# The middle pair of row tiles of batch 0 summed and folded by GpSimd, the outer pair by VectorE, with a new order of the opening's calls

## The chip, the cores and the metric

The kernel runs on one core of one Trainium2 chip. The time is the device time of one launch in microseconds (us): the median of several runs. A profile is one further execution of the same program; its times are given beside it.

## What is computed

```python
# x: 8 x 8 x 512 x 64 (batch, head, row, dim), state: 8 x 8 x 32 x 64
def _attn_ref(x, state):
    scores = scale * np.matmul(x, state.transpose(0, 1, 3, 2))
    ...                                    # softmax over the 32 states: a
    xread = np.matmul(a, state)
    scores2 = scale * np.matmul(state, x.transpose(0, 1, 3, 2))
    ...                                    # softmax over the 512 rows: a2
    sread = np.matmul(a2, x)
    return np.concatenate([xread, sread], axis=2)     # 544 rows a head

def _moe_ref(x, w_ch1, w_ch2):             # x: 8 x 544 x 512
    mixed = np.real(np.fft.fft(np.fft.fft(x, axis=1), axis=2))
    u = x + mixed
    ...                                    # layer norm of u: un
    return u + np.maximum(un @ w_ch1, 0.0) @ w_ch2    # 512 -> 2048 -> 512
```

Heads side by side make the 512 columns. Input and output are f32; the kernel works in bf16 on TensorE.

## The kernel before

The kernel goes through eight batches. Of each batch it makes the attention's reads (xread for 512 rows, sread for 32 state rows), then the Fourier mix, then the layer norm and the two layers of the MLP. The mix is done by matrix products with tables of cosines (TC) and sines (TS). Because cosines are even and sines odd, a row and its mirror image need the same table entry, so the rows are first summed or folded: fewer products remain.

**Recorder and order.** Every engine call goes through a recorder (L21 to L63), which collects the calls into groups and replays the groups in the order that the list ORDER gives (L68 to L132). No scheduler reorders behind it. So each engine and each DMA queue gets its instructions in that order, and each then waits for its own operands only. BANKS (L133 to L140) says in the same way which of six PSUM banks each product takes. All instructions have the helper's line, L63, in the profile, so groups are told apart by tile names.

**The opening.** Batch 0 is written apart (`open_batch`, L718 to L816), as nothing else is there to work on. Its steps: ACT and VectorE cast the loaded state (stb) and x (xin) to bf16; TensorE turns the state (sT, by `turn_state`) and four tiles of x (xTp to xT, by `turn`); `score` makes scores (esp), ACT the exponentials (EE); `read` makes a read of one of four row tiles (xrp, which VectorE scales into XF or XR); `sread` makes the state rows (XQ), which `state_rows` puts into XR through ACT. The four row tiles are rows 0 to 127 and 128 to 255 (XF, k = 0 and 1) and, with rows in reverse, 256 to 383 and 384 to 511 (XR, k = 1 and 0): so the pair k = 1 is the middle pair of row tiles, and the pair k = 0, whose XR also takes the state rows, the outer. Then `even` and `odd` (L804 to L814), both on VectorE and for both pairs at once: Sm is the sum of XF and XR, XE0 are Sm's columns folded by addition, XO0 by subtraction (both are shown as SS, the tile that holds them), and ZB (shown as NN) takes two single columns.

**The mix of batch 0.** `transform(0)` (L841) gives the steps. `begin` opens four accumulators (gp); `low_of` adds products with the state rows (XB), `terms_of(j, part)` products with XE0 and XO0, where `part` is the row pair k; `out_of` copies the sums into G (ACT for even j, VectorE for odd j). `over_d` makes the products along the columns (yp), `add_sums` adds the input and sums for the mean (U), `centre_sums` subtracts the mean (ub), `turn_u` turns the result by TensorE (tp) and copies it into unT, from which the first layer (ph, `layer1`) starts. In the main schedule the calls stand like this, from L1320 on:

```python
    low_of(0, 1), low_of(1, 1)
    state_rows()
    low_of(2, 1), low_of(3, 1)
    even()
    ...
    terms_of(0, 1), terms_of(1, 1)
    odd()
    terms_of(2, 1), terms_of(3, 1)
    terms_of(0, 0)
```

ORDER then decides where each of their calls really lands.

**ACT's tables.** The sine tables TS, TC (`sine_s`, `sine_c`) and TEO (`second_sines`) come from ACT's Sin function, the exponentials from Exp. ACT has to load a table (ACT_TABLE_LOAD) when the next function isn't in the one it holds. The kernel places small calls on a spare tile ("gate") to choose when that happens: a Sin ahead of the state copies, `exp_again` ahead of the exponentials, `sin_table` behind them.

**Fillers.** `warm(n)` issues n small matmuls on zeros.

**Loads.** Batch 0's x comes in parts, two on ACT's queue and the others on SP's (`load_x`); state and the following batches' x are on SP's queue. The weights, w1 and w2 in four quarters each, are issued from GpSimd (`first_weights`, `second_weights`) and are taken by its software queue. `cast_x` and `state_blocks` for batches 1 and 2 run on GpSimd too.

Of the kernel before, what the change touches and what calls it, by code (L numbers as in the profile page):

```python
# [49 lines left out]
class _Engine:  # L50
# [3 lines left out]
    def __getattr__(self, what):  # L54
# [14 lines left out]
        19 62 66 61 9-10 12 1 7 11 2 5 4 3 163 8 49 13 6 298 14 55 15 17 16 50 22 0 75-82 29 143 25 27 26 47 28 38 31 41 23  # L69
        144-145 40 39 32 146-147 30 20 46 21 42 48 148 43-45 149 18 24 34-35 33 37 36 72-74 83-118 130 119 329 120-121 123 122  # L70
        155 131 157 124 156 168 330 172 125 141 170 126 169 171 173 142 176 127-129 133-134 184 178 180 192 68 54 159 69-71 177
        185 193 59-60 58 67 64 316 63 65 187 189 186 135-137 188 138 194 196 195 197 139-140 153-154 216 174 331-332 175 206-210
        212 179 211 181 221 219 213 222 132 150-151 182 152 190 198-199 191 217 214 218 200 263 160 167 201-202 51 265 161
        203-204 267-268 165-166 205 299 162 56 261-262 300 158 264 304 266 297 307 303 302 301 57 228 232 229 220 225-227 224
        233 245 223 244 241 183 215 236-240 252-254 231 235 234 230 276-277 247-248 278-279 246 250-251 259 257 255 269 256 272
        249 242-243 258 271 274 284 270 273 317 312 310 309 319 315 314 313 311 318 280-283 285 290 292-293 291 294 275 286 288
        323 322 287 327 326 320 289 321 328 343 324 341 325 345 339 347 340 348 355 333 337 353 378 351 335 386 354 352 346 387
        361 360 342 338 344 385 379 362-365 367 308 260 366 368 52 296 358 382 381 398 356 390-391 380 383-384 521 392-393 396
        394 439 401 400 399 336 357 359 397 334 402-404 406 405 408 407 409 522 413-414 505 523-524 410 415 412 411 441 525 305
        371 370 369 373 422 374 419 375 426 424 420 423 53 526 421 417-418 459 457 349 376 455 453 461 476 465 388 463 473 469  # L80
        467 460 395 350 440 462 456 454 377 458 464 470 468 466 389 472 488 474 480 518 451 481 445-446 449 482 450 487 484 491
        442 492 447 485 496 475 477-478 443 448 495 500-501 506 429-430 428 427 452 591 493 486 479 483 529 536 497 516 498 489
        517 502 499 490 578 164 306 579 507 503 574 527 504 471 508 372 576 580 528 575 416 577 433 432 435 437 434 431 436 543
        582 512 532 519 530 494 583 514 444 520 531 550 533 539 537 589 509 540 538 560-563 510 555 544 556 545 511 438 546 549
        772 547 553 548 559 552 557 554 584 558 598 592 534 585-586 630 622 600 564 569 567 601 606 614 587-588 593 602-603 573
        568 572 570-571 607-608 596 595 597 594 609-610 621 611 613 612 616-617 625 618 627 626 620 619 604 541 624 632 637 599
        535 551 631 615 605 590 623 638 542 652 677 633 641 639 635 565 634 642 640 636 646 661 668 628 566 653 662 678 647 649
        671 654 648 655 670 663 669 664 684 689 685 690 680 682 650 644 659 672 629 683 658 681 667 651 688 693 645 673 660
        714-715 751 704 736-737 757 761 716-717 701 656 700 740 699 295 698 718 728 727 729 657 730 733 732 731 581 674-675
        694-695 679 767 762 782 708 774-775 768 922 745 744 705 771 742 769 741 746 743 738 752 739 754 756 706 763-764 758 755  # L90
        753 776-777 709 778 783 779-780 791 786 790 794-795 787 789 788 702-703 676 713 796 697 765 818 812 864 784 792 802 797
        804 816 814 871 759 808 719 820 766 813 865 819 793 803 785 798 815 805 817 760 809 821 830 823 711 725 720 710 825 726
        712 707 722 806 810 873 799 828 734 880 837 723 721 826 824 827 735 800 781 801 747-748 849 862 842 831 872 807 874 829
        881 836 835 846 850 838 840 839 841 811 863 845 843 852 870 724 773 770 851 750 844 866 858 856 875 911 832 893 877 884
        882 892 833 883 876 857 696 853 859 867 887-888 919 904 886 902 907 974 908 889-890 912 903 921 665-666 891 822 896 691
        847 895 848 899 898 897 900-901 692 686 643 687 954 932 914 878 909-910 920 894 955 928-929 934 968 834 960 957 959 925
        923-924 879 1102 941-942 970 980 996 963 917 976 905 1035 991 987 939 969 975 997 1046 981 933 906 1036 964 918 992 940
        930 913 931 935 943 916 915 937 944-948 938 971 965 949 966 986 950 977 988 967 953 952 951 978 984 993 1103 927 936 958
        973 926 962 961 956 1047 989 982 1007 985 994 979 990 983 1008 1048 1003 998 1012 1040 1009 1053 1022 1024 1058 1101
        1000 999 1001 1014 1005 1013 1004 1002 1041 1006 1054 1010 1025 1011 1060 1086 1061 1051 1067 1077-1078 1049 1062  # L100
        1015-1016 1063 1023 1059 1018 1027 1052 1064 1070 868 1071 1073-1074 1072 860 869 861 854 1075-1076 855 1079-1080 1050
        1087 1140 1017 1026 1031 1042 1280 1105 1104 1107 515 1134 1139 1137-1138 1106 1082 1037 1097-1098 1055 1119 1146 1084
        1236 1112 1069 1065 1056 1083 1099-1100 1066 1088 1038 1091 1113 1132 1108 1148 1094 1213 1166 1164 1110 1120 1019 1028
        1147 1237 1133 1114 1089-1090 1115-1116 1118 1117 1126 1122 1095 1081 1121 1124 1123 1141 1096 1143 1142 1130 1125 1111
        1144 1158 1205 1154 1092 1193 1162 1168 1127 1160 1149 1032 1085 1214 1165 1043 1109 1159 1167 1155 1206 1093 1194 1169
        1145 1131 1128 1161 1163 1174 1231 1207 1188 1219 1150 1175-1177 1151 1178 1057 1039 1136 1135 513 1179 1232 1220
        1181-1182 1180 1279 995 1020-1021 425 1029 1238-1239 1183 1172 1225 1156 1264 1191 1229 1226 1157 1192 1230 1185 1208
        1173 1171 1186 1189 1240 1184 1241 1190 1187 1243 1201 1196 1224 1197 1281-1282 1129 1068 1153 1200 1285 1195 1283-1284
        1209 1215 1255 1245 1256 1260 1227 1288 1257-1258 1244 1228 1247 1274 1261 1198 1030 1242 1044 1248 1250 1254 1249 1170
        1253 1199 1045 1033-1034 1275-1276 1221 1233 1335 1272 1277 1222 1289 1259 1265 1304 1273 1278 1308 1268 1305 1270  # L110
        1290-1291 1315 1252 1251 1267 1316 1292 1266 1234 1286 1321 1331 1297 1364 1343 1319 1327 1337 1376 1310 1407 1262 1293
        1269 1294 1296 1306 1295 1322 1312 1314 1332 1344 1299 1313 1300 1303 1301 1309 1342 1361 1302 1271 1202 1210 1287 1336
        1298 1320 1328 1216 1377 1365 1395 1408 1311 1338 1333 1325 1339 1359 1329 1340 1334 1326 1330 1317 1354 1402 1390 1360
        1318 1391 1403 1263 1398 1378 1435 1409-1410 1345 1357 1356 1355 1358 1379 1411 1399 1412 1348 1346-1347 1349 1367 1372
        1352 1368 1353 1307 1323 1235 1223 1386 1380 1366 1371 1413 1419 1421 1211-1212 1420 1217 1424-1425 1203-1204 1218 1341
        1423 1422 1369-1370 1392 1404 1426-1427 1416 1400 1362 1446-1447 1396 1384 1350 1428 1436 1429 1440 1393 1405 1363 1373
        1397 1351 1385 1401 1454-1455 1481 1491 1431 1441 1474 1461 1536 1450 1492 1482 1475 1462 1451 1439 1438 1418 1448-1449
        1456-1457 1468 1437 1458 1460 1459 1463 1476 1478 1464 1414-1415 1432 1445 1465-1466 1452 1512 1570 1499 1501 1489 1443
        1453 1477 1467 1444 1430 1497 1493 1469 1479 1537 1442 1513 1500 1490 1502 1498 1494 1472 1470 1473 1480 1516 1483 1507
        1495 1485 1524 1563 1519 1517-1518 1496 1520 1486 1508 1510 1509 1504 1511 1394 1406 1521 1505 1433 1538 1484 1527 1381  # L120
        1532 1525 1514 1564 1387 1528 1434 1515 1506 1523 1539 1522 1544 1554 1567 1558 1556 1550 1557 1540 1546 1471 1526 1531
# [50 lines left out]
def kernel(  # L172
# [545 lines left out]
    def open_batch():  # L718
# [92 lines left out]
        def odd():  # L811
            nc.vector.tensor_sub(XO0[:, :, 0:256], Sm[:, :, 0:256], Sm[:, :, 512:256:-1])
            nc.vector.tensor_sub(XO0[:, :, 256:512], Sm[:, :, 256:0:-1], Sm[:, :, 256:512])
            nc.vector.memset(XO0[:, :, 0:1], 0.0)  # L814
# [740 lines left out]
```

## Time and profile before

| | |
|---|---|
| runs | 288.75, 287.68, 288.82 us; median 288.75 |
| profiled execution | 287.47 us, of which the span of the core's records is 285.7 |
| granted TensorE clock | 0.997 |
| last exponential of batch 0 ends (ACT) | 11.56 us |
| XQ, the state rows before they are turned (VectorE) | 13.49 to 13.78 |
| Sm, both pairs (VectorE) | 15.48, 0.69 us |
| first-axis products gp end (PE) | 19.37 |
| first matmul of layer 1, ph (PE) | 22.39 |
| state 0 has landed | 3.00 |
| tiles of x 0 have landed | 4.34, 5.96, 7.30, 8.34 |
| quarters of w1: issued by GpSimd | 11.59, 15.48, 16.29, 17.02 |
| quarters of w1: landed | 17.49, 21.00, 23.55, 26.08 |

Times inside an execution count from the start of its span. PE is TensorE, DVE VectorE, POOL GpSimd, and SP the engine that issues most of the DMAs. A row of a timeline has the start, the duration, the engine, the operation with output and inputs, and in brackets the idle time before it with what ended it. A row with "x3" stands for three instructions that follow each other without a gap; their durations overlap where an engine pipelines. The chain of work is followed back from the last instruction of the execution to whatever released each step; what is not in it had time to spare.

### The profile page before, as it was taken

To read this page: it belongs to the slowest core of one execution; us is meant where nothing else is said; L and a number is where in the kernel's file an instruction comes from. 1 tells how busy PE (TensorE), PEld (TensorE's weight loads), DVE (VectorE), ACT (ScalarE), POOL (GpSimd) and SP (SyncE) were. 2 spreads that over 40 slices of the span, in tenths; PEclk is the share of its full clock that TensorE was granted. 3 is DMA by queue.
4 is the path that set the end of the run, shared out by engine and by line. 5 is a ranking of instruction groups with operands and counts; after the bars stand their busy time and mean duration, and the time that the engine had idled before them with its cause. 6 is when DMAs were issued, how large, how long until landed. Compare 5 with 4: busy or idle time off the path is not lost.

```text
span 285.7 us, 6835 instructions
## 1 busy us (share of the span) xinstructions
PE 275.2 (96%) x2615; PEld 199.0 (70%) x2644; DVE 210.6 (74%) x554; ACT 162.0 (57%) x327; POOL 92.5 (32%) x227
## 2 busy tenths in 40 slices
PE   7899999999999999999999999999999999999993
PEld 6788985555655778567758777576577667686882
DVE  6877777468899988985798688959766578224892
ACT  7897656746936576368377564586566653254000
POOL 8392476670660033502712119006200028000000
PEclk9999999999999999999999999999999999999998
DMA  8999959966366346861379640413201520978366
GB/s 156 185 181 190 202 95 181 197 146 153 83 157 103 93 116 156 107 170 25 80 169 194 149 94 19 98 53 65 84 0 48 151 65 18 182 149 136 92 162 184
DMA packets 110972, 34.91 MB, mean 122 GB/s; under 512 B 101996, under 2 KB 106476, under 8 KB 110940
## 3 DMA queue, kind: packets, MB, share of 16 engines
q1 hardware_dynamic: 100220, 28.72, 47.5%
q0 software_dynamic: 4224, 4.19, 9.7%
q10 hardware_dynamic: 6496, 1.57, 2.6%
q8 instruction: 20, 0.33, 0.5%
q14 instruction: 12, 0.10, 0.1%
HBM read 22.41 MB, written 14.02 MB: 128 GB/s over the span
## 4 chain that ended last, share of the span: by engine, by line
PE 87%; DVE 7%; DMA 2%; issue 1%; ACT 1%; SPq 1%; DVEq 0%
PE ph L63 39%; PE poA L63 18%; PE poB L63 13%; PE gp L63 4%; PE po L63 3%; PE yp L63 2%; DVE U L63 2%; DMA xs<-in_x_dram 2%; PE esp L63 2%; PE eTp L63 1%; PE xrp L63 1%; DVE XR L63 1%; PE xfp L63 1%; DVE ot L63 1%; SPq L63 1%
## 5 line engine op out<-in xcount | busy, mean ns | idle before, releaser
L63 PE MATMUL ph<-unT,w 128*128 128x512 bf16 (+2 forms) x743 | 127.9, 315 | 1.4
L63 ACT ACTIVATE hT<-ph 128x512 bf16<-128x512 f32 x128 | 72.1, 596 | 76.6 <-PE ph L63 76.3
L63 PEld LDWEIGHTS <-w 128*128 128x128 bf16 x768 | 64.3, 98 | 42.5 <-issue 0.6
L63 PEld LDWEIGHTS <-hT 128*128 128x128 bf16 x632 | 60.4, 98 | 14.8 <-issue 0.3
L63 DVE SCALAR_TENSOR_TENSOR ot<-poA,rstd,U 128x256 f32<-128x256 f32 (+1 forms) x46 | 21.7, 475 | 16.5 <-PE poA L63 13.8
L63 POOL CAST xin<-xs 128x2048 bf16<-128x2048 f32 (+3 forms) x14 | 14.5, 1046 | 48.5 <-PE poA L63 20.3
L63 PE MATMUL poB<-w,hT 128*128 128x256 bf16 x224 | 28.2, 273 | 0.0
L63 POOL TENSOR_TENSOR rstd<-rstd,mhalf 128x1 f32<-128x1 f32 x34 | 20.3, 604 | 1.1
L63 POOL TENSOR_TENSOR rstd<-mv,epst 128x1 f32<-128x1 f32 x14 | 2.8, 211 | 42.9 <-DVE mv L63 42.9
L63 ACT CAST G<-gp 128x288 bf16<-128x288 f32 (+2 forms) x31 | 12.8, 477 | 5.6 <-PE gp L63 5.3
L63 ACT ACTIVATE ub<-U,S 128x512 bf16<-128x512 f32 (+1 forms) x22 | 15.1, 706 | 1.5 <-DVE U L63 1.3
L63 PE MATMUL po<-w,hT 128*128 128x512 bf16 x60 | 15.4, 379 | 0.2
L63 PE MATMUL poB<-TA,SA 128*128 128x256 bf16 x120 | 15.5, 273 | 0.1
L63 PE MATMUL poA<-TA,SB 128*128 128x256 bf16 x120 | 15.6, 273 | 0.0
L63 DVE SCALAR_TENSOR_TENSOR U<-yp,XF 128x2 f32<-128x2 f32 (+1 forms) x24 | 10.0, 419 | 7.5 <-PE yp L63 5.3
L63 DVE SCALAR_TENSOR_TENSOR ot<-poB,rstd,ot 128x256 f32<-128x256 f32 x30 | 14.2, 478 | 1.0 <-PE poB L63 0.8
L63 PE MATMUL poA<-TC,hT 128*128 128x256 bf16 (+1 forms) x120 | 14.5, 265 | 0.1
L63 POOL COPY XT<-XR 32x514 bf16<-32x514 bf16 x7 | 4.2, 605 | 31.8 <-DVE U L63 15.8
L63 PE MATMUL poA<-w,hT 128*128 128x256 bf16 x112 | 14.5, 273 | 0.0
L63 ACT ACTIVATE junk<-U,S 128x512 bf16<-128x512 f32 x20 | 14.3, 716 | 0.2
L63 PE MATMUL poA<-TB,hT 128*128 128x256 bf16 x112 | 14.3, 273 | 0.0
L63 DVE SCALAR_TENSOR_TENSOR ot<-poB,rstd,U 128x256 f32<-128x256 f32 x15 | 7.2, 478 | 9.0 <-PE poB L63 9.0
(197 smaller groups left out, 478.3 us busy)
## 6 DMA issues: line engine op xcount, KB each, us to landing
xs<-in_x_dram SPq DMA_DIRECT2D x22, 256.0 KB, 3.8
w<-in_moe_w_ch_dram POOLq DMA_DIRECT2D x8, 512.0 KB, 6.8
out_dram<-ot SPq DMA_DIRECT2D x15, 256.0 KB, 2.4
r_dram<-ot SPq DMA_DIRECT2D x14, 256.0 KB, 2.4
out_dram<-r_dram SPq DMA_DIRECT2D x14, 256.0 KB, 3.7
xs<-in_x_dram SPq DMA_DIRECT2D x8, 192.0 KB, 4.9
xs<-in_x_dram ACTq DMA_DIRECT2D x2, 256.0 KB, 4.7
l_dram<-ot SPq DMA_DIRECT2D x2, 256.0 KB, 2.0
```

The costliest lines, as they stand in the source:

```text
L63: self._rec.add(self._name, lambda: f(*args, **kw), key)
```

## The change

`even` and `odd` take a row pair k and an engine, and work on that pair alone. The pair k = 1 goes to GpSimd, both folds at once, and the pair k = 0 stays with VectorE:

```diff
-        def even():
-            nc.vector.tensor_add(Sm, XF, XR)
-            nc.vector.tensor_add(XE0[:, :, 128:256], Sm[:, :, 256:128:-1], Sm[:, :, 256:384])
-            nc.vector.tensor_add(XE0[:, :, 0:128], Sm[:, :, 0:128], Sm[:, :, 512:384:-1])
-            nc.vector.tensor_copy(XE0[:, :, 128:129], Sm[:, :, 256:257])
-            nc.vector.tensor_add(ZB[:, 2:4, 0:1], Sm[:, :, 128:129], Sm[:, :, 384:385])
-
-        def odd():
-            nc.vector.tensor_sub(XO0[:, :, 0:256], Sm[:, :, 0:256], Sm[:, :, 512:256:-1])
-            nc.vector.tensor_sub(XO0[:, :, 256:512], Sm[:, :, 256:0:-1], Sm[:, :, 256:512])
-            nc.vector.memset(XO0[:, :, 0:1], 0.0)
+        def even(k, eng):
+            m, e = Sm[:, k], XE0[:, k]
+            eng.tensor_add(m, XF[:, k], XR[:, k])
+            eng.tensor_add(e[:, 128:256], m[:, 256:128:-1], m[:, 256:384])
+            eng.tensor_add(e[:, 0:128], m[:, 0:128], m[:, 512:384:-1])
+            eng.tensor_copy(e[:, 128:129], m[:, 256:257])
+            eng.tensor_add(ZB[:, 2 + k, 0:1], m[:, 128:129], m[:, 384:385])
+
+        def odd(k, eng):
+            m, o = Sm[:, k], XO0[:, k]
+            eng.tensor_sub(o[:, 0:256], m[:, 0:256], m[:, 512:256:-1])
+            eng.tensor_sub(o[:, 256:512], m[:, 256:0:-1], m[:, 256:512])
+            eng.memset(o[:, 0:1], 0.0)
...
-    even()
+    even(1, nc.gpsimd)
+    odd(1, nc.gpsimd)
+    even(0, nc.vector)
...
-    odd()
+    odd(0, nc.vector)
```

This makes 1755 groups of calls where there were 1747, and ORDER and the choice of PSUM banks are written anew. From about 36 us on the order is the old one; the opening's differs. Engine by engine, the two programs differ there like this:

- ACT: the four state copies (stb) and the x cast stand ahead of the Sin on the spare tile, not behind it, and the program has five table loads, not four. Three multiplications that make negative tables stand ahead of the copy that puts the state rows into XR. The last load, for Exp, stands ahead of the second half of TEO and the copies into G, not behind them.
- VectorE: the casts of two further tiles of x 0 stand ahead of the sT and xT copies. The first unT copy stands behind an addition for the second tile of U.
- TensorE: the tiles of x are turned before the first scores, and the reads run in the order 2, 3, 1, 0, with 1 and 0 behind the last exponential. The transposes of batch 1's state stand ahead of yp.
- GpSimd: ahead of its part of XB come two casts of x 1 and two quarters of w1; behind it the fold of the pair k = 1 with a third quarter of w1 in it, then the state copies, casts and the mirror table, then the state copies for batch 2, the last quarter of w1 and the first of w2.
- SP: state 1 is loaded earlier, the parts of x 1 come in another order, and the load of state 2 stands behind those of x 2, the first of which waits for a cast on GpSimd.

## The prediction

> **What bounds the kernel now.** I read the busy times first, then the chain that ended last, then the opening engine by engine.
>
> ```profile
> PE 275.2 (96%) x2615; PEld 199.0 (70%) x2644; DVE 210.6 (74%) x554; ACT 162.0 (57%) x327; POOL 92.5 (32%) x227
> ...
> PE 87%; DVE 7%; DMA 2%; issue 1%; ACT 1%; SPq 1%; DVEq 0%
> ```
>
> PE is busy for 275.2 us of 285.7. Its own idle times sum to 5.8 us before the last matmul, 3 of them before 9 us; after the first layer-1 matmul (ph, 22.39) there are only some 2 us (the largest 0.38 at 28.0 and 0.56 at 49.84). So later matmuls don't wait, and the change, which touches only the first 36 us, acts through one thing: when the opening hands PE its steady work. The chain's steps from 0 to 27 us (start, duration):
>
> ```profile
> 3.60 4.75 DMA xs<-in_x_dram
> ...
> 10.06 0.78 PE esp L63 x22
> 12.09 0.70 DVE XR L63
> 13.56 0.23 DVE XQ L63
> 13.83 0.70 PE warm L63 x6
> 14.54 1.59 PE gp L63 x13
> ...
> 16.84 2.53 PE gp L63 x29
> 19.37 0.22 PE warm L63 x4
> 19.59 0.47 PE yp L63 x4
> 20.09 0.71 DVE U L63 x2
> 21.99 0.36 DVE unT L63
> 22.39 1.05 PE ph L63 x16
> ```
>
> The chain runs through scores (esp), exponentials, reads (XR), state rows (XQ), the sums gp and yp. The fold that is moved lies just before the gp row of 16.84. ACT's own timeline of the opening:
>
> ```profile
> 1.90 1.28 ACT L63 ACT_TABLE_LOAD   x1 [1.90 <-issue]
> ...
> 5.78 0.54 ACT L63 ACTIVATE TC<-gen,halfpi 128x288 bf16<-128x288 f32 x1
> 6.32 1.28 ACT L63 ACT_TABLE_LOAD   x1
> 7.61 0.20 ACT L63 ACTIVATE gate<-gate 128x1 f32<-128x1 f32 x1
> 8.24 0.59 ACT L63 COPY xT<-xTp 128x512 bf16<-128x512 bf16 x1 [0.43 <-PE xTp L63]
> 9.81 1.75 ACT L63 ACTIVATE EE<-esp 128x512 bf16<-128x512 f32 x3 [0.48 <-PE esp L63]
> ```
>
> ACT has 0.43 + 0.48 us of idle between the gate and the last exponentials, so it is nearly a bound here already: its last exponential ends at 11.56.
>
> **ACT: one more table load (the largest term).** In the changed program the first ACT work is the four state copies and the x cast; the sine activation that stood ahead of them comes after. So a load of another table stands ahead of the copies, behind their wait for the state (landing at 3.00), and the sine table is loaded after them: five loads instead of four. Before, the first load ran at 1.90 under the wait for data and cost nothing. Stepped with the rows: 3.0 + 1.28 load, four copies of 0.30 to 5.5, cast 0.62 to 6.2, load 1.28 to 7.5, gate, TS and TC to 8.6, load 1.28 to 9.9, gate to 10.1. Before, this point was 7.61 + 0.20 = 7.81. Of the +2.3, 0.9 goes into the idle above. Then xT 10.1, four exponentials at a spacing of 0.5 from 10.6: the last ends at 12.7 (+1.15). The Trainium skill ("ScalarE: Activation LUTs", section "What ACT_TABLE_LOAD costs") puts some 1.38 us of draining onto each load. The rows show none: TC ends at 6.32, where the load starts, and the gate follows at 7.61. By the row the extra load is 1.28, by the rule 2.66 and the exponentials +2.5; I take the row, since this is the same instruction in this place.
>
> **VectorE's order.** The casts of x tile 1 and of the 96-row tile (landings 7.30 and 8.34) now stand ahead of the sT copy, which ends at 9.27 instead of 8.09. Scores wait for sT, so this alone would put the last exponential at 12.0 (+0.43). It lies beside ACT's delay: the later counts, so nothing is added.
>
> **PE's order.** Reads go 2, 3, 1, 0, and reads 1 and 0 both stand behind the last exponential, ahead of sread: about +0.2. XQ ends at 15.1 against 13.78 (+1.36). The transposes of the next batch's state take the place of the four warm matmuls before yp (0.22 each way): nothing.
>
> **The fold.** VectorE's Sm add, two folds and two odd folds fall from two row tiles to one: 0.69 + 2 x 0.25 + 2 x 0.38 become about half. GpSimd gets the other half. It has no such row; the nearest are its two-input adds:
>
> ```profile
> 29.10 0.66 POOL L63 TENSOR_TENSOR XEl<-XT 32x256 f32<-32x256 bf16 x1
> ```
>
> 0.66 for 256 columns, with 0.45 for 128 (XQl<-XEl at 31.50): some 1.8 ns a column and 0.2 fixed. So Sm (514) takes 1.1, two of 128 take 0.9, two of 256 take 1.3, small ones 0.2: 3.5 us. The lower end is 2.5 (all bf16, where the row writes f32), the upper 5 (locked, below). It starts when XF and XR of tile 1 are there, 14.6, and with a weight DMA issue (0.75) and copies between ends at 19.1. PE wants the pieces at 18.2 to 21.5 in my stepping, 0.45 to 1.5 us after each is done. That cover hides it; without it each us of lateness is a us at the end.
>
> The Trainium skill ("SBUF — State Buffer", section "Who interferes with whom") speaks against this: a VectorE operation with two SBUF inputs and a GpSimd operation that reads SBUF shut each other out. The trace agrees:
>
> ```profile
> 172.42 0.68 DVE L63 TENSOR_TENSOR hT<-hT 128x1024 bf16<-128x1024 bf16 x1
> 172.46 1.17 POOL L63 TENSOR_TENSOR XEl<-XT 32x256 f32<-32x256 bf16 x1
> ```
>
> XEl takes 1.17 instead of 0.66 under it; the VectorE row keeps its 0.68 here, and in three such overlaps takes 0.75 to 0.79. In the opening VectorE's own fold (some 1 us of two-input work) meets GpSimd's reads. By the unlocked row the cost is 0; by the rule all of the overlap, 1 us, is lost on one of the two. GpSimd's part fits in the slack up to about 0.5, so I take +0.3, from 0 to +1.
>
> **ACT behind the fold.** The copy that makes the state rows waits for GpSimd's Sm and minus operations and three ACT multiplies now precede it (XR 15.9 to 16.5, before 14.84 to 15.44); the exp table load moves from behind the G copies to ahead of them (18.1 to 19.3, before 19.53), so ub isn't later by it. PE's low gp runs 15.6 to 17.6, then the terms 18.2 to 20.5 (before to 19.37), yp ends at 21.45 (before 20.06: +1.4).
>
> **After yp.** U starts at 21.5 (+1.4); unT now stands behind a U operation of the second tile on VectorE, so the first ph starts at 24.1 (+1.7). That is partly made up: by the 192nd ph the lag is +1.3, by the 231st +1.2.
>
> **The DMAs that are moved.** On GpSimd two casts of x and two w1 quarters go ahead of XB, one w1 quarter stands amid the fold, the last behind the state blocks of batch 2, which wait for a state load behind the x(2) loads on SP's queue; each holds the next. The last w1 quarter lands at 32 to 34 (before 26.08), wanted at about 35.3 (before 34.3); the first two quarters of w2 at 34 to 36 and 40, wanted at 40 and 42.2. So cost 0, with 1.3 to 3 us of slack; a queue later by 2 would turn into a stall on w1 of 0.7 or more. The opening's own loads on SP change places but none that PE waits for lands later by the step.
>
> **Sum.** Lag +1.2 to +1.7 at steady work, I take +1.3, and +0.3 for the shared port: +1.6, own range +1.0 to +2.2. Nothing behind can take it in but the waits of about 0.9 named above. The profiled execution then is 287.47 + 1.6 = 289.1 (span 287.3), and as the median of before is 1.28 above its profiled execution, the forecast is 288.75 + 1.6 = 290.35.
>
> **The rivals.** B, absorbed: the extra load delays the exponentials, but the waits of 0.38 at 28.0 and 0.56 at 49.84 vanish, since what ends them is not delayed. For it: PE's first hundred ph catch up 0.4 in my stepping. Against: the waits after 22.39 are for things that hang on the same chain. It gives +0.6: 289.3.
>
> C, GpSimd becomes the bound: folds at the locked price (5 us instead of 3.5) end 1.5 after their time, and eat the slack of 0.45 at the first piece; the lag grows by 1.0 to 1.5, or the last w1 quarter comes late by the same. For it: the 1.17 row and four things queued behind each other. Against: the VectorE part is only 1 us long. It gives +2.9: 291.65.
>
> D, not slower: GpSimd starts tile 1's fold before the state rows are there, so that PE's gp terms start without the fillers (0.70 at 13.83, 0.11 at 16.13, 0.11 of idle before 16.84): -0.8 at most. It decides if the last exponential ends no more than 0.8 us after 11.56, that is if the first table load runs before the state has landed and its sine load hides in the wait for x (xT is only there at 8.24). Time 288.75 - 0.8 = 287.95 with no lag, 288.75 with 0.8. Against: the order of the instructions, which puts the second load behind the cast.
>
> **How the numbers follow.** A measurement of this kernel can tell about 0.5% from no change, 1.44 us. A (forecast, 290.35) 0.52, B 0.18, C 0.23, D 0.07. The bound for slower is 290.19: two thirds of A (0.34) and all of C make 0.57; the rest of A (0.18), B and a quarter of D make 0.38; what of D gains more than its fillers, 0.05. The range takes B less 0.7 (runs of before differ by 1.1) and C plus 0.75: 288.6 to 292.4; outside are D's faster part and a lock or a late quarter worse than C.
>
> **What would show it.** ACT: five loads, the second sine load near 6.2 to 7.5, the last EE ends near 12.7. DVE: sT near 9.3. POOL: Sm<-XF,XR 128x514 near 1.1 us; much over 1.5 says lock. PE: yp near 21.4, first ph near 24.1, and no wait over 0.3 at the last w1 quarter near 35. It would be wrong if the first load ran at 1.9 without waiting, if the copies shared the sine table, or if the folds took over 5 us.

## The result, and the profile after

The changed kernel takes 290.42 us in the median of 5 runs (290.17 to 291.48), where the kernel before took 288.75 in runs beside it. The medians differ by 1.67 us; the ratio of the runs is 1.0093 with a 95% interval of 1.0072 to 1.0114. A second set of both kernels on one chip gave 290.23 against 287.95, ratio 1.0076 (1.0061 to 1.0091), or 2.2 us. The forecast was +1.6 us (0.55%) and 290.35: the sign is right and the time lies in the range, but by both ratios the loss is larger, by some 0.6 us in the second set. That 290.42 lies so near to 290.35 is in part luck. The forecast was counted from the 288.75 of the kernel before, and in three later sets the medians of that kernel were 287.70 to 287.95.

The profiled execution took 291.48 us, the slowest of the five, with a span of 289.7. The page's busy times and the shares of its chain:

```profile
span 289.7 us, 6847 instructions
PE 276.5 (95%) x2615; PEld 199.2 (69%) x2644; DVE 213.0 (74%) x554; ACT 163.1 (56%) x328; POOL 96.6 (33%) x235
...
PE 69%; POOL 7%; SPq 5%; issue 4%; DVE 4%; DMA 4%; ACT 4%; POOLq 0%; DVEq 0%; ACTq 0%
```

PE's work is nearly the same; the chain has more of other engines in it. Its steps of the opening (start, duration):

```profile
0.72 2.58 DMA gen<-in_state_dram
...
3.37 1.28 ACT L63
...
6.55 1.28 ACT L63
...
8.81 1.28 ACT L63
...
10.78 1.98 ACT EE L63 x4
...
15.23 1.15 POOL Sm L63
...
16.76 0.60 ACT XR L63
17.36 0.02 issue
17.38 0.44 DVE Sm L63
...
17.84 1.35 DVE SS L63 x3
...
20.19 0.30 PE gp L63
...
25.16 1.05 PE ph L63 x16
```

Before, the chain began with the loads of x. In this execution it begins with the load of the state, and goes through three table loads on ACT. Then it passes GpSimd's Sm, ACT's copy into XR, VectorE's Sm and folds. A further execution of the same program, the second profile (span 288.5), has another chain up to ACT's copy:

```profile
4.37 4.33 DMA gen<-in_state_dram
...
8.84 0.29 POOL stb L63
...
13.36 0.65 POOL XB L63
...
14.22 1.16 POOL Sm L63
...
15.76 0.59 ACT XR L63
...
16.38 0.44 DVE Sm L63
...
19.18 0.30 PE gp L63
```

It begins with the landing of batch 1's state at 8.70 and follows GpSimd's queue: casts of batch 1's state and x, w1 issues, its part of XB, Sm. ACT's own list (last exponential, table load, two sines, three multiplications) ends at 15.70 in this execution, and GpSimd's clearing of XB at 15.75; the copy starts at 15.74. So two paths reach this copy almost together, one along ACT and one along GpSimd's queue, and taking time out of one alone leaves the other. ACT and PE show the waits that matter, in the first profile:

```profile
3.37 1.28 ACT L63 ACT_TABLE_LOAD   x1 [3.37 <-DMA gen<-in_state_dram]
...
10.68 2.07 ACT L63 ACTIVATE EE<-esp 128x512 bf16<-128x512 f32 x4
```

```profile
20.19 0.30 PE L63 MATMUL gp<-NN,SS 128*128 128x288 bf16 x1 [0.66 <-DVE SS L63]
```

The first row is the new table load, held by the state's landing; the second has the four exponentials in one block, now without idle time ahead of them. The third is a wait that the kernel before did not have: PE waits for a fold piece of VectorE (0.51 in the second profile).

Milestones of the opening, read from one trace of each kernel (us; "XQ" is its end; "last x cast" is the start of the cast of the 96-row tile, "gp" the end of the first-axis products, "ph" the first matmul of layer 1):

| kernel | state lands | last x cast | last EE ends | XQ | gp | ph |
|---|---|---|---|---|---|---|
| before | 3.00 | 8.46 | 11.56 | 13.78 | 19.37 | 22.39 |
| changed, first profile | 3.30 | 8.63 | 12.75 | 15.55 | 22.02 | 25.16 |
| changed, run again | 2.84 | 8.51 | 12.29 | 14.69 | 21.02 | 24.16 |
| Sin first | 2.88 | 8.28 | 11.78 | 14.21 | 20.69 | 23.83 |
| fold on VectorE | 3.01 | 8.37 | 12.54 | 15.20 | 21.60 | 24.74 |
| order only | 2.91 | 8.46 | 11.96 | 14.40 | 21.09 | 24.22 |
| even first | 3.16 | 8.17 | 12.61 | 15.29 | 20.93 | 24.28 |
| mended | 3.13 | 8.54 | 11.96 | 14.54 | 20.37 | 23.30 |
| load alone | 2.83 | 8.21 | 12.16 | 14.05 | 19.69 | 22.70 |
| fold alone | 2.87 | 8.25 | 11.35 | 13.61 | 20.76 | 25.45 |
| fold, casts ahead | 2.98 | 8.38 | 11.48 | 13.70 | 20.86 | 24.82 |
| released copy | 2.94 | 8.35 | 12.51 | 14.88 | 21.24 | 24.38 |
| released copy, Sin first | 3.15 | 8.18 | 11.59 | 14.19 | 20.57 | 23.50 |
| before, XB work ahead | 2.90 | 8.35 | 11.45 | 13.67 | 19.21 | 22.21 |

### The profile page after: what moved, and what is told of

Read it like the earlier page. It is cut to its first block, busy times and chain, and to the rows that moved or that the text cites. A ratio compares the mean times of both kernels' runs of the same rounds, so it can differ in the third digit from the quotient of the medians.

```text
span 289.7 us, 6847 instructions
## 1 busy us (share of the span) xinstructions
PE 276.5 (95%) x2615; PEld 199.2 (69%) x2644; DVE 213.0 (74%) x554; ACT 163.1 (56%) x328; POOL 96.6 (33%) x235
## 4 chain that ended last, share of the span: by engine, by line
PE 69%; POOL 7%; SPq 5%; issue 4%; DVE 4%; DMA 4%; ACT 4%; POOLq 0%; DVEq 0%; ACTq 0%
PE ph L63 30%; PE poA L63 17%; PE poB L63 13%; SPq L63 5%; DMA xs<-in_x_dram 3%; PE gp L63 3%; POOL xin L63 2%; PE yp L63 2%; ACT L63 1%; POOL stb L63 1%; DVE ot L63 1%; DVE XR L63 1%; DMA gen<-in_state_dram 1%; PE eTp L63 1%; PE esp L63 1%
```

## The experiments

The theory after the first trace was: the table load, and VectorE's folds stretched by GpSimd's. The first rival: only the load. A second, which came up on the way: the new order of the calls, apart from both. Every ratio is to the kernel before on the same chip.

**The changed kernel again.**

> The changed kernel once more, unaltered, so that the others can be compared with it on the same chip and with a second profile. The first profile had the first ph 2.8 us later than before (25.16 against 22.39), and the same lag at the end but for 0.8. If that is the kernel and not the one execution, this profile shows the first ph at 24.8 to 25.2 and the ratio to before is 1.007 to 1.010. Rival (the profiled execution was an outlier): first ph near 24.1 as forecast, ratio 1.005.

Median 290.23 against 287.95, ratio 1.0076 (1.0061 to 1.0091); ph at 24.16. So two executions of one program differ by 1.0 us at this point, and the first profile was on the late side. Of that, 0.46 is the state's landing (3.30 against 2.84). The last exponential ends 9.45 us after that landing in both. Another 0.40 lies between the last exponential and XQ. There VectorE's copy XB takes 0.71 instead of 0.29, where GpSimd's copy of the same size had started 0.04 ahead of it. The last 0.14 lies between XQ and the end of gp. The rival was right on the place of ph, the theory on the ratio.

**The Sin first.** The edit, in ACT's part of ORDER:

```diff
-        33 35-36 34 37 24 72-74
+        24 33 35-36 34 37 72-74
```

> The changed kernel with one call moved back: ACT's Sin on the spare tile stands again ahead of the four state copies, so the program has four table loads. My theory (the table load behind the wait for the state costs 1.15 us at the exponentials, less what VectorE's order of casts holds back by itself, 0.43): the first load at about 2 us, the last exponential ends at 12.0 to 12.1 instead of 12.75, first ph 0.7 earlier than in the changed kernel, total 0.7 less (289.7 where before is 288.75, ratio about 1.003). Rival (the load is covered, the whole loss is in the fold): nothing moves, ratio 1.006.

289.51 against 287.81, ratio 1.0075 (1.0048 to 1.0103). The last exponential ends at 11.78 instead of 12.29 and ph comes 0.33 earlier than in the second profile of the changed kernel. So the last exponential gained 0.51, and the ratio did not move. This is a miss for the theory. The 0.33 at ph cannot be put down to the load either: GpSimd's Sm, too, starts 0.33 earlier (13.89 against 14.22), as batch 1's state landed earlier here, and the chain of this execution runs along GpSimd's queue, as in the second profile. What the load costs in the changed kernel is not shown by this run, since the other path held. ACT's row of the exponentials:

```profile
9.68 2.10 ACT L63 ACTIVATE EE<-esp 128x512 bf16<-128x512 f32 x4 [0.91 <-PE esp L63]
```

With the load gone, ACT waits 0.91 us for scores. In the new order sT stands behind the last x cast, and all tiles are turned ahead of the first scores. In the four kernels with the new order and four loads the last exponential ends 3.4 to 3.5 us after the last x cast starts, in before 3.1. Two of the four (released copy with the Sin first, and mended) have sT ahead of that cast again, and still end 3.41 and 3.42 after it, against 3.50 in the other two. So sT's place is worth some 0.08. The rest fits the place of the scores behind the turn of the last tile: before, one exponential ran at 8.73 and three at 9.81 (1.75 us), now all four run in a row (2.10 us). With five loads the bound is the other one, 9.45 to 9.57 after the state's landing.

**The fold given back to VectorE.**

```diff
-    even(1, nc.gpsimd)
-    odd(1, nc.gpsimd)
+    even(1, nc.vector)
+    odd(1, nc.vector)
```

> The changed kernel in its new order, but the fold of the middle pair is given back to VectorE; five table loads stay. My theory after the trace (GpSimd's adds keep their time and VectorE loses: its four folds take 0.52, 0.29, 0.70 and 0.74 where the twice as wide ones took 0.29 and 0.42; the state rows' copy also waits for GpSimd's Sm): VectorE's folds go back to 0.25 to 0.4 each, the ZB and XB work of GpSimd ends before 15 and the copy into XR starts about 16.2 instead of 16.75; PE's first ph comes 0.8 to 1.5 us earlier than in the changed kernel, ratio to before about 1.002. Rival (only the load counts): VectorE has 0.7 us more to do, ratio 1.006 to 1.008.

290.16 against 287.81, ratio 1.0075 (1.0061 to 1.0089): no gain. The stretching is real. VectorE's rows in the changed kernel's first profile:

```profile
15.58 1.09 DVE L63 TENSOR_SCALAR gen<-gen 128x512 int32<-128x512 int32 x1
...
17.84 1.35 DVE L63 TENSOR_TENSOR SS<-Sm 128x128 bf16<-128x128 bf16 x3
...
19.20 0.74 DVE L63 TENSOR_TENSOR SS<-Sm 128x128 bf16<-128x128 bf16 x1
```

GpSimd's, beside them:

```profile
15.23 1.16 POOL L63 TENSOR_TENSOR Sm<-XF,XR 128x514 bf16<-128x514 bf16 x1 [0.63 <-DVE rcs L63]
...
18.37 0.67 POOL L63 TENSOR_TENSOR SS<-Sm 128x256 bf16<-128x256 bf16 x1
...
19.25 0.60 POOL L63 TENSOR_TENSOR SS<-Sm 128x256 bf16<-128x256 bf16 x1
```

And VectorE with GpSimd's adds taken away:

```profile
15.23 0.38 DVE L63 TENSOR_SCALAR gen<-gen 128x512 int32<-128x512 int32 x1
...
18.15 0.28 DVE L63 TENSOR_TENSOR SS<-Sm 128x256 bf16<-128x256 bf16 x1
...
19.30 0.22 DVE L63 TENSOR_TENSOR SS<-Sm 128x128 bf16<-128x128 bf16 x1
```

The integer operation takes 0.38 instead of 1.09, a 128-column fold 0.22 instead of 0.74, while GpSimd's rows are near what the prediction took from its unlocked rows (1.1 for Sm). But VectorE then has twice the work, and its last piece is as late: from its last Sm to its last fold piece 2.74 us, against 2.76 in the first profile. Nor is the stretch undone in full. With its adds gone, GpSimd's two casts of x 1 come forward to 16.16 and lie beside VectorE's two Sm adds, of which the second takes 0.83 (0.43 in the second profile). So the run shows that giving the work back gains nothing; what the stretch alone costs it does not separate.

**Both undone.**

> The changed kernel with both suspects undone: the Sin stands ahead of the copies again (four table loads), and the fold of the middle pair is on VectorE. What is left is the new order of the calls. My theory: load and fold are not all; last exponential at 11.8 (held by sT), the three multiplications ahead of the copy into XR, VectorE's last folds behind the odd ones and 16 transposes between the two yp still cost, together 0.9 to 1.5 us: first ph at 23.3 to 23.8, ratio 1.003 to 1.006. Rival (load and fold are the whole loss): first ph at 22.4 to 22.8, ratio 1.000 to 1.001.

290.23 against 287.95, ratio 1.0086 (1.0065 to 1.0108), ph at 24.22. The theory did not expect this: with four loads and no GpSimd fold the new order still costs what the change costs. But it does not show the new order by itself. This order is made for a VectorE with half the fold: from its last Sm to its last piece VectorE takes 3.17 us here. And GpSimd's casts of x 1 have again moved into the gap that its fold left:

```profile
15.83 1.51 POOL L63 CAST xin<-xs 128x512 bf16<-128x512 f32 x2
```

```profile
16.02 0.83 DVE L63 TENSOR_TENSOR Sm<-XF,XR 128x514 bf16<-128x514 bf16 x1
```

This Sm takes 0.83 and the fold of 128 columns behind it 0.63, where alone they take 0.43 and 0.22: some 0.8 us on VectorE's list, which PE then waits for. So sharing between the two engines is in this test too, through other calls. The late scores belong to the order alone (the last exponential at 11.96, +0.40), and so does the place in VectorE's list of the piece that PE waits for; how much of the 1.8 at ph the order makes by itself is not shown.

**The load alone**, in the kernel before:

```diff
-        24 34-35 33 37 36 72-74
+        34-35 33 37 36 24 72-74
```

> The kernel before with one call moved: ACT's Sin on the spare tile stands behind the four state copies and the x cast. This adds the table load behind the wait for the state and nothing else. My theory: first load at about 3.0 to 3.3, ACT reaches the exponentials 2.3 us later, 0.9 of it absorbed by its idle times, last exponential at 12.7 to 13.0, first ph and total +1.2 to +1.4, ratio 1.0045. Rival by the rule on draining (each load costs 2.66): last exponential at 14, ratio 1.009. Rival (absorbed): ratio 1.000 to 1.001.

288.26 against 287.81, ratio 1.0015 (1.0006 to 1.0024). The expected 1.0045 is out. ACT's rows:

```profile
2.90 1.28 ACT L63 ACT_TABLE_LOAD   x1 [2.90 <-DMA gen<-in_state_dram]
...
5.97 1.28 ACT L63 ACT_TABLE_LOAD   x1
...
10.10 2.06 ACT L63 ACTIVATE EE<-esp 128x512 bf16<-128x512 f32 x4
...
14.99 0.60 ACT L63 CAST XR<-warm 32x512 bf16<-32x512 f32 x1 [0.22 <-issue]
```

The last exponential ends 0.6 later than before, but the copy into XR starts only 0.15 later (before: 14.84). Before, ACT idles 0.67 ahead of this copy, for a GpSimd clearing that stands behind a cast of another batch's state. This is that row of before:

```profile
14.84 0.60 ACT L63 CAST XR<-warm 32x512 bf16<-32x512 f32 x1 [0.67 <-POOL XB L63]
```

For the copy, that idle time took most of the delay. PE's path takes in less: XQ ends 0.27 later than before, since before the chain between the last exponential and XQ ran through VectorE's reads, and this step takes 1.89 here instead of 2.22. From there PE carries 0.3 on to ph and to its last ph, and the total is 0.45 later. A load costs its 1.28; a load of 2.66, as the rule on draining has it, would have shown at the exponentials, and did not.

**The fold alone**, in the order of before: the change's code, with GpSimd's eight calls put behind the last read of its pair, a w1 quarter ahead, one inside and one behind.

> The kernel before, in its own order of the opening, with the fold of the middle pair on GpSimd from the time that its reads are there (two weight transfers stand inside and behind it, one is issued earlier). No further table load. My theory (the shared port): VectorE's Sm and folds overlap GpSimd's and each stretches by 0.3 to 0.45 us, so that the end of the sums is 0.3 to 1.0 later in spite of half the work, ratio 1.001 to 1.004. Rival (the fold is a gain that the new order spoils): VectorE ends its part 0.7 earlier, PE's products start without fillers, ratio 0.998.

292.12 against 287.81, ratio 1.0129 (1.0107 to 1.015), the slowest of all. Its runs fall into two groups, 290.63 and 290.78 in one and four from 292.08 to 292.16 in the other; the profile is of the first, so some 1.4 us of the median's loss are in no trace and stay open. VectorE and GpSimd start their Sm within 0.4 us:

```profile
15.48 1.04 DVE L63 TENSOR_TENSOR Sm<-XF,XR 128x514 bf16<-128x514 bf16 x1 [0.49 <-ACT XR L63]
```

```profile
15.08 1.16 POOL L63 TENSOR_TENSOR Sm<-XF,XR 128x514 bf16<-128x514 bf16 x1 [0.23 <-DVE XF L63]
```

VectorE needs 1.04 for half the Sm that takes 0.69 whole in before. PE then waits for GpSimd's pieces:

```profile
17.19 0.24 PE L63 MATMUL gp<-NN,SS 128*128 128x144 bf16 x1 [0.27 <-POOL SS L63]
18.29 0.24 PE L63 MATMUL gp<-NN,SS 128*128 128x144 bf16 x1 [0.80 <-POOL SS L63]
```

gp ends 1.4 late; then PE waits 1.6 more for x casts that stand on GpSimd behind the fold. In the old order, in this kernel and the next, rival C of the prediction is true: GpSimd's folds are the bound.

**The fold alone, x casts ahead of the last w1 quarter.**

> The fold alone in the order of the kernel before, once more, with GpSimd's three casts of x 1 directly behind its fold and the last w1 quarter behind them. In the first version the products ended 1.4 later than before (20.76 against 19.37), and the transposes of x 1 then waited 1.6 for casts that stood behind two weight transfers. My theory: the second part goes (first ph at 23.8 to 24.0 instead of 25.45, ratio 1.005), the first, which is the fold's own, stays. Rival (the casts are not what is waited for): first ph stays above 25, ratio 1.011 or more.

290.20 against 287.70, ratio 1.0078 (1.006 to 1.0097). The 1.4 to 1.5 at gp stays, as expected; of the second part about half goes, since the state casts behind the x casts are now late: from gp to ph PE loses 0.94 instead of 1.67, and ph at 24.82 misses the expected 23.8 to 24.0. Against the profiled time of the fold alone, 290.63, this kernel's profile is only 0.3 faster. PE's waits from 15 to 26 us (engine, what it waited for, us in total, times, longest):

```profile
PE sTp L63 <- POOL stb L63: 1.3, 1, 1.3
PE gp L63 <- POOL SS L63: 1.1, 2, 0.8
```

**Released copy into XR.** In the changed kernel, GpSimd's groups 202 and 204 ahead of its Sm (236), VectorE's integer operation (132) ahead of 151.

> The changed kernel with GpSimd's ZB subtraction and XB clearing put ahead of its Sm, so that ACT's copy into XR no longer waits behind Sm, and VectorE's integer operation on 512 columns (1.09 us under GpSimd's Sm, 0.38 when GpSimd does not read) put ahead of the reads. My theory (the chain through GpSimd's Sm, ACT's copy and VectorE's Sm is real): XR copy 0.5 earlier, VectorE's Sm 0.5 earlier at 16.8 instead of 17.4, total 0.4 to 0.6 less than the changed kernel, ratio 1.006. Rival (the folds end last anyway): 0 to 0.1.

290.17 against 287.95, ratio 1.0074 (1.0059 to 1.0089), the same as the changed kernel on that chip. A miss. The copy starts at 15.83, no earlier than the 15.74 of the second profile, and now it is held by ACT's own multiplications; VectorE's Sm starts at 16.44 and its first three fold pieces take 1.95. GpSimd's path is off the chain, and ACT's, which had been level with it, holds the copy in its place.

**The same with the Sin first, sT ahead of the last cast, unT ahead of the second U.**

> As the last one, with the Sin ahead of the copies (four loads), VectorE's sT copy ahead of the last cast as in the kernel before, and the first unT copy ahead of the second tile's U. GpSimd keeps the fold. My theory (load 0.7 to 1, release 0.5, sT 0.3, unT 0.2): first ph at 22.8 to 23.2, ratio 1.001 to 1.003, still not better than before because VectorE's folds stretch under GpSimd's. Rival (the shared port costs nothing once the order is mended): ratio below 0.999.

289.30 against 287.95, ratio 1.0048 (1.0033 to 1.0063); ph at 23.50. About 0.9 less than the changed kernel, though less than expected. Both paths to ACT's copy are shortened here at once, where the Sin first and the released copy, each alone, gained nothing. That fits two paths that end together; as four edits were made in one run, it is not shown which of them counted. PE still waits 0.57 for a fold piece.

**The even half first.** In VectorE's part of ORDER, in the changed kernel:

```diff
-        246 260-262 248 245 247
+        246 245 247 260-262 248
```

> The changed kernel with VectorE's own fold put in another order: the second half of XE0 and its single column ahead of the two subtractions for XO0, as the products of the outer pair want them. My theory: in all kernels with the new order TensorE waits 0.5 to 0.66 us for exactly this piece (its products end 1.9 us after the last fold piece in each of them), so the wait goes and the first ph comes 0.4 to 0.6 earlier than in the changed kernel run again (23.6 to 23.8 against 24.16), ratio about 1.006. Rival (the subtractions then come late and take the wait's place): 0 to 0.1.

289.85 against 287.70, ratio 1.0067 (1.0046 to 1.0088). PE's wait is gone; the chain is PE's own from the last read on:

```profile
15.35 0.70 PE warm L63 x6
16.05 1.96 PE gp L63 x16
...
18.65 0.74 PE gp L63 x10
19.39 0.06 PE warm L63
19.45 1.48 PE gp L63 x17
```

From XQ to the end of gp it takes 5.64 us, where before took 5.59 and the changed kernel 6.33 to 6.47. So with VectorE's pieces in the order in which they are wanted, this stretch of the opening is as long as before in this execution; in the mended kernel, with the same order, it is 5.83. In this execution exponentials and reads were late (state at 3.16), so ph is at 24.28; the total is lower by less than the interval, which neither shows nor rules out the expected 0.5. The mended kernel below differs by this same edit from the one with the released copy and the Sin first: there ph is 0.20 earlier and the ratio lower by 0.0009, also within the intervals.

**All of it.**

> All that was found so far in one kernel, GpSimd keeping its fold: four table loads, sT ahead of the last cast, GpSimd's ZB and XB work ahead of its Sm, VectorE's integer operation ahead of the reads, the even half of the outer pair first, the first unT ahead of the second U. My theory: 0.4 to 0.5 less than the version without the last edit (1.0048), first ph at 23.0 to 23.1, ratio 1.003: not better than before, since VectorE's two-input operations still stretch under GpSimd's. Rival (GpSimd's fold is worth the 0.5 that VectorE no longer does): ratio 1.000 or below.

288.97 against 287.70, ratio 1.0039 (1.0026 to 1.0052), ph at 23.30. About half of the loss is taken back by moving single calls, with GpSimd's fold kept; the expected 1.003 and ph at 23.0 to 23.1 were not reached. What is left at ph, 0.91, lies at the last exponential (+0.40, in part its last x cast, 0.1 late), from there to XQ (+0.36) and from XQ to the end of gp (+0.24), less 0.1 behind it. The other half of this profile's lag arises behind the first ph: it is 1.89 at the last ph.

**The kernel before, with GpSimd's XB work ahead of the cast.**

```diff
-        51 265 161 203-204 267-268
+        51 203-204 265 161 267-268
```

> The kernel before with one GpSimd cast (batch 1's state, waiting for its load to 14.28) and one small clearing moved behind the ZB addition and XB clearing, for which ACT's copy into XR waits 0.67 us. Fold on VectorE as before. My theory: the copy starts about 14.4 instead of 14.84 and VectorE's Sm at 15.2, when its last read is scaled, instead of 15.48: total 0.2 to 0.3 less, ratio 0.999. Rival (the products wait for their tables): 1.000.

287.61 against 287.70, ratio 0.9992 (0.9985 to 1.0000). The copy starts at 14.51 instead of 14.84:

```profile
14.51 0.60 ACT L63 CAST XR<-warm 32x512 bf16<-32x512 f32 x1 [0.45 <-DVE XR L63]
```

It beats the changed kernel clearly, and the kernel before by 0.1% at the edge of what can be told.

## Why the prediction was right in sign and too small

The forecast's lag, step by step, beside the two profiles of the changed kernel:

| step | forecast | run again | first profile |
|---|---|---|---|
| last exponential | +1.15 | +0.72 | +1.18 |
| from there to XQ | +0.2 | +0.2 | +0.6 |
| XQ to the end of gp | -0.2 | +0.74 | +0.88 |
| gp to the first ph | +0.6 | +0.12 | +0.12 |
| first ph to the end, port included | -0.1 | +1.0 | +1.2 |
| sum, on the span | +1.6 | +2.8 | +4.0 |

**The table load** was placed rightly: five loads, the first held by the state, the second sine load at 6.1 to 7.8, the exponentials at 12.3 to 12.75. The row's price of 1.28 held, the rule's 2.66 did not. What the forecast didn't see is that "nothing behind can take it in" is false for the load by itself: the copy into XR lost only 0.15 of the 0.6, and the total 0.45. The term put at 0.43 beside it is there when the load goes (11.96 in the kernel with both undone: +0.40), so its size was right. Its cause was not: sT's place on VectorE is worth some 0.08, and the rest goes with PE turning all tiles ahead of the scores, a term that the forecast does not have. Up to ACT's copy into XR (forecast 15.9, second profile 15.74) the stepping held.

**The fold** is the term that was sized wrongly. The forecast stepped GpSimd's pieces (3.5 us in sum; the trace has 3.7) against PE's needs, found slack, and took +0.3 for the port on top, judging it by GpSimd's slack. GpSimd was on time indeed, and it was VectorE that lost: in the second profile its first three folds take 1.35 and the fourth 0.74. Two things make PE's wait of 0.5 to 0.66 together. One is this stretch. The other is the order of VectorE's own pieces: the second half of XE0 stands behind both subtractions, and PE wants it ahead of them. With the unstretched times (the same seven pieces take 1.04 in the kernel with the fold on VectorE) the last piece would be done near 17.9 in the second profile, an estimate, where PE wants it near 18.5; measured it is done at 19.13. So by this estimate PE would not have waited without the stretch; and in the two kernels with the other order it did not wait at this piece in spite of it. Stepping VectorE's list with the stretched times would have shown the wait.

**From gp to ph** it is 0.12, not 0.6: unT does stand behind a U operation, but U itself starts 0.71 after the end of gp, not 1.0 as stepped.

**The later waits.** The two waits that the forecast gives as 0.38 at 28.0 and 0.56 at 49.84 are 0.21 at 28.40 and 0.39 at 50.45 in the trace of before. The first is gone in every kernel with the new order. The second grows to 0.59 or 0.60 in all of them, while both stay as they were in the four other kernels with the opening of before: so about 0.2 of the loss behind ph comes with the new order.

**After ph** the forecast expected a catching up by 0.4 and no loss later. The catching up was 0.2 (192nd ph +1.56 in the second profile). Later 0.45 were lost on a transposing DMA; this is PE's row at 70 us in the second profile:

```profile
70.39 0.29 PE L63 MATMUL esp<-sT,xT 128*128 128x64 bf16 x4 [0.45 <-DMA xT<-xin]
```

This DMA had been issued at 66.75 and landed at 70.35. The one behind it landed at 71.80, 3.15 after its counterpart before (68.65), while PE was 1.6 late: SP's queue had lost more than PE. Another 0.4 to 0.5 is between the last ph and the end. Which of these other losses belong to the new order and which to the execution is not settled: kernels with an early ph lose more behind it (1.0 in mended, 0.55 in the second profile, 0.16 in the order alone), the first profile has its late wait at 85 us (0.40) instead, and the load-alone kernel keeps its +0.31 unchanged to the last ph.

**The weights** were right: the last w1 quarter landed at 31.2 and 32.5 in the two profiles (forecast 32 to 34), and no wait of PE was for it.

**The rivals.** B (absorbed) is true of the load by itself in part, and in another place: the two later waits stay in the load-alone kernel. It is not true of the change. C is true of the fold in the old order only. D (a gain) was never there: PE's fillers ahead of the products stayed, and in the even-first kernel the time from XQ to gp is before's. The likeliest case came near by a sum in which some terms were too high and others too low: in the second profile 0.43 and 0.48 less at two steps, 0.94 and 1.1 more at two others. That the time came out so near is luck in this respect too.

## What to carry to other kernels

Where a change comes with a new order of calls, undo the named parts and keep the order: here that kept the whole loss, and neither named part would have told. Look then at what slid into the gap: with the fold gone, GpSimd's casts came forward and stretched VectorE's adds in its stead. Where two paths end together, undoing either shows nothing; undo both. Step every engine's list of pieces in the order in which their consumer takes them, also the engine that gets less work, and with the durations that it has beside the other engine: here neither the order nor the stretch made the wait by itself. And a delay upstream is to be followed to the next wait that is for something else: a load of 1.28 us came out as 0.6 at the exponentials and 0.45 in the total.

## What the runs showed of the hardware that was not expected

GpSimd's Sm (1.16 us) and fold pieces (0.60 to 0.67) took in the changed kernel what the forecast had from rows without overlap, and VectorE's operations beside them were stretched, also those with one input: a 128x512 integer operation from 0.38 to 1.09 us, the 32x514 copy XB from 0.29 to 0.71 where GpSimd's copy of the same size had started just ahead. At 172 us in the kernel before it was the other way round. In each of these pairs the operation whose row starts first kept its time. The Trainium skill ("SBUF — State Buffer", section "Who interferes with whom") has that as its rule, and also names copies and one-input operations on VectorE; the prediction used only the part on two inputs. By the rows' starts not all pairs follow it: at 19.2 in the first profile VectorE's fold starts at 19.20 and GpSimd's at 19.25, and VectorE's is the one that is stretched (0.74 instead of 0.22). Nor does GpSimd always keep its time: its two casts of x 1 took 1.51 instead of 1.17 beside VectorE's Sm in the kernel with the order alone.
